# Queries and keys laid out chunk by chunk, and the row of maxima turned by VectorE

## The chip, the cores and the metric

The kernel runs on one core of one Trainium2 chip. What counts is the device time of one launch in microseconds, the median of the runs. A core has five engines with a queue of instructions each: TensorE (PE, with its weight loads shown apart as PEld), VectorE (DVE), ScalarE (ACT), GpSimd (POOL) and SyncE (SP), which here issues most DMAs. Sixteen DMA engines move what is issued.

## What is computed

Attention with hashed buckets comes first, and its output runs through a mixture of experts and a gated two-layer network. The change lies in the attention.

```python
B, H, S, D = q.shape                       # 2, 8, 768, 64
q_bits = (np.einsum('bhsd,dk->bhsk', q, proj) > 0).astype(np.int64)
k_bits = (np.einsum('bhsd,dk->bhsk', k, proj) > 0).astype(np.int64)
...
mask = q_bucket[:, :, :, None] == k_bucket[:, :, None, :]
scores = scale * np.matmul(q, k.transpose(0, 1, 3, 2))
scores = np.where(mask, scores, -1000000000.0)
scores = scores - np.max(scores, axis=-1, keepdims=True)
attn = np.exp(scores)
attn = attn / (np.sum(attn, axis=-1, keepdims=True) + 1e-09)
return np.matmul(attn, v).astype(np.float32)
...
x = _moe_ref(x=x, **moe_kwargs)
return _moe2_ref(x=x, **moe2_kwargs)
```

## The kernel before

There are 16 heads (batch times heads) of 768 queries and 768 keys each; 768 is six chunks of 128. For each head four tiles of 128 partitions by 768 columns hold the operands: `X` (queries in rows 0 to 63, 12 rows of bucket bits, and in row 76 the row of maxima), `K2` (keys and bits, with -1 in row 76), `Y` and `K1` (the high and low halves that make the product exact). Four such sets take turns.

Each head goes through two kinds of steps, both in chunks of 128.

`mx(n)` takes one chunk of queries as the stationary operand: two matmuls of 384 columns (line 425) give scores of 128 queries against all keys, and VectorE reduces each to a maximum per query (line 428). The stationary operand is `st["X"][0:76, c::NC]`, every sixth column, so chunk c holds the queries 6p + c for p from 0 to 127. After the sixth chunk one more reduction (line 431) writes the maxima of the head into `top`, with p on the partitions and c in the columns, and SP issues one DMA (line 432) that writes them into row 76 of `X` as one row in the order of the queries.

`scores(k)` takes a chunk of keys as the stationary operand: for each half of the queries (384 columns) line 442 multiplies the halves and line 443 adds the rest, with the row of maxima among it. ScalarE takes the exponential (line 444); it reads the 384 columns of PSUM with a stride of six, so that its output stands chunk by chunk. The tiles in PSUM that scores write into are two. Then ScalarE or VectorE rounds to half precision (`high`), GpSimd or VectorE forms the remainder (`low`), and `pv` (lines 470 to 472) multiplies both with v, 36 small matmuls at a time.

A loop over 96 steps (16 heads times 6) sets the order of everything: in step k come `scores(k)`, then `mx(k + 8)`, and in every odd step `pv` of two earlier steps. So in even steps the two matmuls of line 425 are followed directly by line 442 of the next step, and in odd ones by line 470. Work that comes once per head or per four heads is put between by a table of due steps: loads of queries and keys (`load_r`, line 348), loads of v (`load_v`, line 550) and their maxima on VectorE (`vmax`, line 554), the split into high and low parts (`prep`, lines 359 to 377, with six DMAs), the bucket bits (`bits`, line 398; `put_bits`, lines 383 and 384), and the products of v with the gate (`vgate`, line 531). Each engine and SP's queue run their instructions in that order; an SP instruction that waits holds back all later ones.

Of the kernel before, what the change touches and what calls it, by code (L numbers as in the profile page):

```python
# [9 lines left out]
F32 = mybir.dt.float32  # L10
F32R = mybir.dt.float32r
F16 = mybir.dt.float16
I32 = mybir.dt.int32
AF = mybir.ActivationFunctionType
# [5 lines left out]
P = 128  # L20
B, H, S, D = 2, 8, 768, 64
NH = B * H
BITS = 6
NC = S // P
HS = S // 2
# [17 lines left out]
SC = 2.0**-17  # L43
# [20 lines left out]
def moe_attention_kernel(ctx, tc, qk, v, vt, pj, wg, w1, w2, win, wout, out, cap):  # L64
    nc = tc.nc
    pe, act, dve, pool, sp = nc.tensor, nc.scalar, nc.vector, nc.gpsimd, nc.sync
# [3 lines left out]
    def opened(stack, name, bufs, side="left", **kw):  # L70
        return stack.enter_context(tc.tile_pool(name=name, bufs=bufs, side=side, reuse_waits="tile", **kw))

    def f32(t):
        return t.bitcast(F32)
# [229 lines left out]
    with ExitStack() as actx:  # L304
        pa = opened(actx, "pa", 1)
# [26 lines left out]
        pool.memset(b3, 3.0)  # L332
        rt, b_t = {}, {}
        nm = pa.tile([P, NH, NC], F32, tag="nm", name="nm")
        top = pa.tile([P, NH, NC], F32R, tag="top", name="top")
        mxs = [pa.tile([P, NC, 3], F32, tag=f"mx{i}", name=f"mx{i}") for i in range(2)]
        for t in mxs:
            dve.memset(t[:, :, 2:3], -0.5)
# [80 lines left out]
        def mx(n):  # L419
            h, c = divmod(n, NC)  # L420
            st = sets[h % 4]
            mm = mxs[h % 2]
            for n in range(2):
                ps = ps_m.tile([P, 512], F32, tag="m", name=f"psm{h}{c}{n}")
                pe.matmul(  # L425
                    ps[:, :HS], st["X"][0:76, c::NC], st["K2"][0:76, n * HS : (n + 1) * HS], start=True, stop=True
                )
                dve.tensor_reduce(out=mm[:, c, n : n + 1], in_=ps[:, :HS], axis=AX.X, op=ALU.max)  # L428
            if c == NC - 1:

                dve.tensor_reduce(out=top[:, h], in_=mm, axis=AX.X, op=ALU.max)
                sp.dma_start(out=f32(st["X"])[76:77, :].rearrange("o (p c) -> o p c", c=NC), in_=f32(top)[:, h])

        def scores(k):
            h, j = divmod(k, NC)
            st = sets[h % 4]
            pf = pf_t[k] = pt.tile([P, S], F32, tag="pf", name=f"pf{k}", bufs=4)
            kc = slice(j * P, (j + 1) * P)
            for n in range(2):
                ps = ps_t.tile([P, 512], F32, tag="t", name=f"pst{k}{n}")  # L440
                qc = slice(n * HS, (n + 1) * HS)
                pe.matmul(ps[:, :HS], st["K1"][:, kc], st["Y"][:, qc], start=True, stop=False)  # L442
                pe.matmul(ps[:, :HS], st["K2"][0:77, kc], st["X"][0:77, qc], start=False, stop=True)  # L443
                act.activation(  # L444
                    pf.rearrange("k (c n p) -> k c n p", c=NC, n=2)[:, :, n],
                    ps[:, :HS].rearrange("k (p c) -> k c p", c=NC), AF.Exp, scale=0.125 / SC / SC,
                )

        def high(k, eng):
            phi_t[k] = pt.tile([P, S], F16, tag="phi", name=f"phi{k}", bufs=6)  # L450
# [249 lines left out]
        st, r0 = sets[0], rt[0]  # L700
# [3 lines left out]
        for n in range(2):  # L704
            for i, t in enumerate(("X", "K2")):
                c = slice(n * HS, (n + 1) * HS)
                ps = (ps_m, ps_t)[i].tile([P, 512], F32, tag="mt"[i], name=f"psf{n}{i}")
                pe.matmul(
                    ps[D : D + 12, :HS], pj_sb[i * D : (i + 1) * D, 12 * i : 12 * i + 12], r0[i * D : (i + 1) * D, c],
                    start=True, stop=True,  # L710
# [10 lines left out]
        for n in range(NC):  # L721
            mx(n)
            if n in DOT:
                next(b0)
# [48 lines left out]
        for g in range(1, G):  # L773
            b = 4 * NC * (g - 1)
# [11 lines left out]
        for h in range(NH):  # L786
            k = NC * h + NC - 1 + LAG
# [52 lines left out]
        h = NH - 1  # L840
# [242 lines left out]
    def heat(n):  # L1083
# [21 lines left out]
        out=gates, in0=ps2[:, :, NW:], scalar=1.0 / LS, in1=gates, op0=ALU.mult, op1=ALU.add  # L1105
# [368 lines left out]
```

## Time and profile before

| | us |
|---|---|
| median of the runs (three) | 677.33 |
| lowest and highest run | 677.24, 678.81 |
| time of the profiled execution | 675.88 |
| its span | 674.1 |
| busy in the span: TensorE, VectorE, ScalarE, GpSimd | 638.4, 481.0, 426.6, 229.8 |

The profile is of one execution. The attention fills the first 240 us of the span; the rest are the experts and the two-layer network. A matmul's record reaches from its start to a modelled end, and records of neighbours overlap, so the distance between starts tells more than a duration. A busy share is an average over stages with different limits.

### The profile page before, as it was taken

Reading aid. Unit: us, or ns where it says so; the run is one execution under the profiler, and the core shown is the slowest. Engines: PE = TensorE matmul, PEld = TensorE weight load, DVE = VectorE, ACT = ScalarE, POOL = GpSimd, SP = SyncE. Lnnn points to the kernel's source line nnn. Section 1 sums busy time; section 2 is a strip of 40 time slices with the busy share of each in tenths; the row PEclk is TensorE's granted clock in tenths of the full one; section 3 lists DMA queues with packets and bytes.
Section 4 is the critical chain, followed back from the end, with each engine's and each line's share of the span. In section 5 each row is a group of like instructions: output and inputs, shape, how many; then the busy total and the mean of one; then the engine's idle time right before and its main releaser. Section 6 shows DMA issues by size and latency. Waiting matters only on the chain.

```text
span 674.1 us, 14367 instructions
## 1 busy us (share of the span) xinstructions
PE 638.4 (95%) x5518; PEld 479.7 (71%) x5518; DVE 481.0 (71%) x1038; ACT 426.6 (63%) x869; POOL 229.8 (34%) x199
## 2 busy tenths in 40 slices
PE   7899999999999769999999999999999999999894
PEld 2588889989899638999999997555555555555541
DVE  6768898898999957888888877888888452222320
ACT  3467778778787826776667765455445576555730
POOL 4339769769778233221077500000000021000011
PEclk9889999999999978999999999999999999999998
DMA  8584764764465065777677735443442011000011
GB/s 236 127 233 115 231 177 122 233 169 109 126 160 165 25 217 193 250 246 257 213 253 228 243 115 162 137 145 126 150 134 92 0 48 48 1 0 1 1 41 59
DMA packets 37840, 94.14 MB, mean 140 GB/s; under 512 B 7576, under 2 KB 13720, under 8 KB 37760
## 3 DMA queue, kind: packets, MB, share of 16 engines
q1 hardware_dynamic: 34672, 85.71, 42.7%
q0 software_dynamic: 2400, 7.36, 3.2%
q8 instruction: 46, 0.75, 0.4%
q14 instruction: 34, 0.28, 0.1%
q10 hardware_dynamic: 688, 0.03, 0.1%
HBM read 67.14 MB, written 6.29 MB: 109 GB/s over the span
## 4 chain that ended last, share of the span: by engine, by line
PE 75%; DVE 10%; DMA 6%; ACT 5%; issue 2%; SPq 0%; POOL 0%; POOLq 0%; ACTq 0%; DVEq 0%
PE psg L1249 16%; PE pso L1276 15%; PE psh L1006 11%; PE psy L1033 11%; PE psm L425 5%; PE pst L442 4%; PE pst L443 3%; DVE mx L428 2%; DMA out_dram<-os,inv 2%; PE psv L470 2%; PE psv L471 2%; PE psv L472 2%; PE psg L531 2%; DMA vr<-in_v_dram 1%; ACT junk L1203 1%
## 5 line engine op out<-in xcount | busy, mean ns | idle before, releaser
L458 POOL TENSOR_TENSOR plo<-pf,phi 128x768 f16<-128x768 f32 x86 | 147.1, 1736 | 60.4 <-ACT phi L452 24.9
L444 ACT ACTIVATE pf<-pst 128x384 f32<-128x384 f32 x192 | 83.5, 486 | 47.4 <-PE pst L443 45.7
L428 DVE TENSOR_REDUCE mx<-psm 128x1 f32<-128x384 f32 x192 | 96.3, 548 | 20.0 <-PE psm L425 19.7
L1291 POOL DMA_INDIRECT out_dram<-os,inv x12 | 12.1, 1008 | 270.8 <-DVE os L1283 244.5
L163 DVE SCALAR_TENSOR_TENSOR wl<-raw,wh 128x1024 f16<-128x1024 f32 (+1 forms) x68 | 82.7, 1218 | 6.3 <-ACT wh L157 5.2
L1249 PE MATMUL psg<-yTh,ch 128*128 128x512 f16 (+1 forms) x256 | 83.4, 326 | 3.2 <-DVE rl L1252 3.2
L1249 PE MATMUL psg<-yTl,ch 128*128 128x512 f16 (+1 forms) x256 | 83.4, 326 | 0.0
L1249 PE MATMUL psg<-yTh,cl 128*128 128x512 f16 (+1 forms) x256 | 83.4, 326 | 0.0
L1252 DVE SCALAR_TENSOR_TENSOR rl<-rl,psg 128x512 f32<-128x512 f32 x64 | 35.0, 551 | 64.4 <-ACT rl L1251 64.0
L442 PE MATMUL pst<-Y,K 128*128 128x384 f32 x192 | 75.2, 392 | 2.0 <-ACT pf L444 2.0
L1249 PEld LDWEIGHTS <-ch 128*128 128x128 f16 x512 | 50.0, 98 | 35.9
L452 ACT ACTIVATE phi<-pf 128x768 f16<-128x768 f32 x85 | 71.7, 844 | 1.9
L1276 PE MATMUL pso<-ch,gh 128*128 128x512 f16 x192 | 72.8, 379 | 0.0
L1276 PE MATMUL pso<-ch,gl 128*128 128x512 f16 x192 | 72.8, 379 | 0.0
L1276 PE MATMUL pso<-cl,gh 128*128 128x512 f16 x192 | 72.8, 379 | 0.0
L425 PE MATMUL psm<-K,X 76*128 76x384 f32 x192 | 66.8, 431 | 4.6 <-DVE mx L428 3.8
L157 ACT ACTIVATE wh<-raw 128x1024 f16<-128x1024 f32 (+1 forms) x68 | 67.6, 999 | 0.5 <-issue 0.4
L1276 PEld LDWEIGHTS <-gh 128*128 128x128 f16 x384 | 37.6, 98 | 42.3
L443 PE MATMUL pst<-X,K 77*128 77x384 f32 x192 | 66.5, 346 | 0.0
L1033 PE MATMUL psy<-hh,wl 128*128 128x224 f16 x256 | 66.3, 259 | 0.0
L1033 PE MATMUL psy<-hh,wh 128*128 128x224 f16 x256 | 66.3, 259 | 0.0
L1033 PE MATMUL psy<-hl,wh 128*128 128x224 f16 x256 | 66.3, 259 | 0.0
(231 smaller groups left out, 1495.2 us busy)
## 6 DMA issues: line engine op xcount, KB each, us to landing
raw<-in_w_dram SPq DMA_DIRECT2D x64, 512.0 KB
rc<-in_win_dram SPq DMA_DIRECT2D x16, 512.0 KB
rc<-in_wout_dram SPq DMA_DIRECT2D x16, 512.0 KB
r<-in_qk_dram SPq DMA_DIRECT2D x16, 384.0 KB
K<-hi SPq DMA_DIRECT2D x31, 192.0 KB
vr<-in_v_dram SPq DMA_DIRECT2D x4, 768.0 KB
vt<-in_vt_dram SPq DMA_DIRECT2D x8, 384.0 KB
Y<-hi SPq DMA_DIRECT2D x16, 192.0 KB
```

The lines of the kernel that those rows point to most:

```text
L163: dve.scalar_tensor_tensor(out=wl[e, i][:, c : c + n], in0=r, scalar=(S1, S2)[i // 2], in1=wh[e, i][:, c : c + n], op0=ALU.mult, op1=ALU.s ...
L425: pe.matmul(ps[:, :HS], st["X"][0:76, c::NC], st["K2"][0:76, n * HS : (n + 1) * HS], start=True, stop=True)
L428: dve.tensor_reduce(out=mm[:, c, n : n + 1], in_=ps[:, :HS], axis=AX.X, op=ALU.max)
L442: pe.matmul(ps[:, :HS], st["K1"][:, kc], st["Y"][:, qc], start=True, stop=False)
L443: pe.matmul(ps[:, :HS], st["K2"][0:77, kc], st["X"][0:77, qc], start=False, stop=True)
L444: act.activation(pf.rearrange("k (c n p) -> k c n p", c=NC, n=2)[:, :, n], ps[:, :HS].rearrange("k (p c) -> k c p", c=NC), AF.Exp, scale=0 ...
L452: act.activation(phi_t[k], pf_t[k], AF.Copy)
L458: eng.tensor_tensor(out=plo_t[k], in0=pf_t.pop(k), in1=phi_t[k], op=ALU.subtract)
L1006: pe.matmul(ps, l[:, c], r[:, k], start=n == 0, stop=n == 3 * KD - 1)
L1033: pe.matmul(ps, l, r, start=n == 0, stop=n == 3 * KF - 1)
L1249: pe.matmul(ps, l, x, start=n == 0, stop=n == 3 * KD - 1)
L1276: pe.matmul(po[blk][s], l, r, start=first and n == 0, stop=last and n == 2)
```

## The change

The host lays queries and keys out so that column c x 128 + p of a head is token 6p + c: each chunk of `X` is now contiguous, and v is loaded in the same order of keys. So the stationary operand of the maxima is `st["X"][0:76, c * P : (c + 1) * P]`, and the exponential reads PSUM and writes its tile contiguously. The row of maxima must now stand chunk by chunk as well. VectorE turns `top` in blocks of 32 x 32 into one of two tiles `tt`, after which chunk c of the block b lies in partition 32b + c; four DMAs of six partitions with 32 values each carry it into row 76. For that `top` is 26 columns wider and set to zero once.

```diff
-        top = pa.tile([P, NH, NC], F32R, tag="top", name="top")
+        top32 = pa.tile([P, NH * NC + 32 - NC], F32R, tag="top", name="top")
+        dve.memset(f32(top32), 0.0)
+        top = top32[:, : NH * NC].rearrange("p (h c) -> p h c", c=NC)
+        turned = [pa.tile([P, 32], F32, tag=f"tt{i}", name=f"tt{i}") for i in range(2)]
...
-                    ps[:, :HS], st["X"][0:76, c::NC], st["K2"][0:76, n * HS : (n + 1) * HS], start=True, stop=True
+                    ps[:, :HS], st["X"][0:76, c * P : (c + 1) * P], st["K2"][0:76, n * HS : (n + 1) * HS], start=True, stop=True
...
                 dve.tensor_reduce(out=top[:, h], in_=mm, axis=AX.X, op=ALU.max)
-                sp.dma_start(out=f32(st["X"])[76:77, :].rearrange("o (p c) -> o p c", c=NC), in_=f32(top)[:, h])
+                t = turned[h % 2]
+                dve.transpose(t, f32(top32)[:, h * NC : h * NC + 32])
+                rows = f32(st["X"])[76:77, :].rearrange("o (c b i) -> o b c i", c=NC, b=4)
+                for b in range(4):
+                    sp.dma_start(out=rows[:, b], in_=t[32 * b : 32 * b + NC, :])
...
-                act.activation(
-                    pf.rearrange("k (c n p) -> k c n p", c=NC, n=2)[:, :, n],
-                    ps[:, :HS].rearrange("k (p c) -> k c p", c=NC), AF.Exp, scale=0.125 / SC / SC,
-                )
+                act.activation(pf[:, qc], ps[:, :HS], AF.Exp, scale=0.125 / SC / SC)
...
-    qk = np.concatenate([q.transpose(0, 1, 3, 2), k.transpose(0, 1, 3, 2)], axis=2).reshape(NH, P, S)
-    vv = v.reshape(NH, NC, P, D).transpose(2, 0, 1, 3).reshape(P, NH * NC * D)
-    vt = v.reshape(NH // 2, 2, S, D).transpose(0, 1, 3, 2).reshape(NH // 2, P, S)
+    qk = np.concatenate([q.transpose(0, 1, 3, 2), k.transpose(0, 1, 3, 2)], axis=2).reshape(NH, P, P, NC)
+    qk = qk.transpose(0, 1, 3, 2).reshape(NH, P, S)
+    vv = v.reshape(NH, P, NC, D).transpose(1, 0, 2, 3).reshape(P, NH * NC * D)
+    vt = v.reshape(NH // 2, 2, P, NC, D).transpose(0, 1, 4, 3, 2).reshape(NH // 2, P, S)
```

The order of the instructions on TensorE, ScalarE and GpSimd stays as it was. It changes at two places per head. The first is SP's queue; here it is head 1, whose set holds `X_141`, before the change (a row is line, operation, out<-in and size):

```order
L348 DMA r_335<-in_qk_dram 128x768
L520 DMA vt_365<-in_vt_dram 128x768
L348 DMA r_367<-in_qk_dram 128x768
L432 DMA X_141<-top 1x128x6
L348 DMA r_448<-in_qk_dram 128x768
L376 DMA K_147<-lo_311 64x768
L377 DMA Y_146<-lo_311 64x768
L348 DMA r_485<-in_qk_dram 128x768
L550 DMA vr_547<-in_v_dram 128x1536
```

The same place of SP's queue in the changed kernel, whose lines stand a few further down:

```order
L351 DMA r_342<-in_qk_dram 128x768
L524 DMA vt_372<-in_vt_dram 128x768
L351 DMA r_374<-in_qk_dram 128x768
L439 DMA X_141<-tt_159 1x6x32 x4
L351 DMA r_459<-in_qk_dram 128x768
L379 DMA K_147<-lo_318 64x768
L380 DMA Y_146<-lo_318 64x768
L351 DMA r_496<-in_qk_dram 128x768
L554 DMA vr_558<-in_v_dram 128x1536
```

Where one DMA stood there are four, and the loads of r and v behind them keep their order.

The second place is VectorE's queue at the end of the maxima of head 1, before the change:

```order
L428 TENSOR_REDUCE mx_158<-psm_433 128x1
L428 TENSOR_REDUCE mx_158<-psm_436 128x1
L431 TENSOR_REDUCE top<-mx_158 128x6
L679 SCALAR_TENSOR_TENSOR vh_396<-vr_176,sc_353,vh_396 128x6x64
L683 MEMSET vh_396 128x6
```

And in the changed kernel:

```order
L431 TENSOR_REDUCE mx_161<-psm_440 128x1
L431 TENSOR_REDUCE mx_161<-psm_443 128x1
L434 TENSOR_REDUCE top<-mx_161 128x6
L436 STREAM_TRANSPOSE tt_159<-top 128x32
L683 SCALAR_TENSOR_TENSOR vh_403<-vr_179,sc_360,vh_403 128x6x64
L687 MEMSET vh_403 128x6
```

The transposition stands right behind the reduction that it reads, and nothing else moved.

## Rows read from the trace of the kernel before

**Rows 1.** Stretches of 10 us from 50 to 240: sum, busy us of each engine.

```profile
sum 190.00, PE 180.51 PEld 162.27 DVE 169.24 ACT 150.45 POOL 139.31; mean PE 9.50 PEld 8.54 DVE 8.91 ACT 7.92 POOL 7.33
```

**Rows 2.** Groups by line: shapes, count | busy us, mean ns | idle before, releaser.

```profile
L444 ACT ACTIVATE pf<-pst 128x384 f32<-128x384 f32 x192 | 83.5, 486 | 47.4 <-PE pst L443 45.7 <-POOL plo L458 0.8
...
L425 PEld LDWEIGHTS psm<-K,X 76*128 76x128 f32 x192 | 53.3, 313 | 12.3 <-DVE mx L428 8.7 <-ACT hi L359 2.1 <-issue 0.8
L443 PEld LDWEIGHTS pst<-X,K 77*128 77x128 f32 x192 | 37.3, 194 | 0.0
...
L992 ACT ACTIVATE xh<-psa 128x448 f16<-128x448 f32 x8 | 4.3, 543 | 10.2 <-PE psa L989 9.7
```

**Rows 3.** Timeline of TensorE's matmuls: start us, us, engine, line, operands, count.

```profile
148.40 0.62 PE L425 MATMUL psm<-K,X 76*128 76x384 f32 x2
148.86 0.43 PE L442 MATMUL pst<-Y,K 128*128 128x384 f32 x1
...
149.51 0.34 PE L443 MATMUL pst<-X,K 77*128 77x384 f32 x1
149.69 0.62 PE L425 MATMUL psm<-K,X 76*128 76x384 f32 x2
150.16 0.21 PE L470 MATMUL psv<-vh,phi 128*128 128x73 f16 x1
```

**Rows 4.** Timeline of ScalarE, the exponential of the same step.

```profile
148.30 0.49 ACT L444 ACTIVATE pf<-pst 128x384 f32<-128x384 f32 x1 [0.65 <-PE pst L443]
```

**Rows 5.** Timeline of the weight loads, the next one of line 442.

```profile
148.84 0.19 PEld L442 LDWEIGHTS pst<-Y,K 128*128 128x128 f32 x1
```

**Rows 6.** Chain of waits in order of time: start us, us, what.

```profile
54.72 0.45 PE psm L425 x2
...
123.25 0.55 PE psm L425
...
217.58 0.45 PE psm L425 x2
```

**Rows 7.** Groups by line, VectorE, the last reduction of a head.

```profile
L431 DVE TENSOR_REDUCE top<-mx 128x6 fp32r<-128x18 f32 x16 | 2.8, 172 | 0.5
```

**Rows 8.** Timeline of SP's queue around heads 1 and 13.

```profile
27.43 0.79 SPq L383 DMA_DIRECT2D X<-b  x1
...
35.57 0.53 SPq L432 DMA_DIRECT2D X<-top  x1
36.14 0.59 SPq L348 DMA_DIRECT2D r<-in_qk_dram  x1
...
38.68 0.56 SPq L550 DMA_DIRECT2D vr<-in_v_dram  x1
...
194.87 0.51 SPq L432 DMA_DIRECT2D X<-top  x1
```

**Rows 9.** Stretches: busy us, then granted clock, DMA share and GB/s.

```profile
28.00:30.00 2.00, 2.00 (x7) 1.28 (x5) 0.10 (x1) 1.18 (x2) 0.96 (x2) 0.50 1.06 218
...
32.00:34.00 2.00, 2.00 (x13) 1.83 (x13) 1.97 (x6) 0.00 (x0) 0.00 (x0) 0.90 0.07 25
...
36.00:38.00 2.00, 2.00 (x7) 1.36 (x6) 0.35 (x2) 1.93 (x4) 0.00 (x0) 0.50 1.02 373
```

**Rows 10.** Timeline of VectorE, the maxima of v.

```profile
48.67 1.01 DVE L554 TENSOR_REDUCE am<-vr 128x1 f32<-128x384 f32 x2 [1.39 <-DMA vr<-in_v_dram]
```

**Rows 11.** Stretches after the issue of head 15's row, columns as in rows 9.

```profile
219.10:220.20 1.10, 0.97 (x10) 0.64 (x6) 1.03 (x5) 0.71 (x3) 0.00 (x0) 1.00 0.00 0
220.20:220.50 0.30, 0.15 (x1) 0.15 (x2) 0.30 (x2) 0.30 (x2) 0.00 (x0) 1.00 0.26 10
```

**Rows 12.** Timeline of TensorE, the first reader of head 13's row.

```profile
198.34 0.34 PE L443 MATMUL pst<-X,K 77*128 77x384 f32 x1
```

**Rows 13.** Timeline of TensorE, the wait ahead of 26 us.

```profile
26.14 0.56 PE L425 MATMUL psm<-K,X 76*128 76x384 f32 x1 [1.68 <-DVE mx L428]
```

**Rows 14.** The page's row of TensorE's granted clock in 40 slices, in tenths.

```profile
PEclk9889999999999978999999999999999999999998
```

## Prediction

> **What bounds the kernel now.** I read the profile in this order: the table of engines by stretch, the groups of instructions by line, the timeline of TensorE in one step, and the chain of work that ended last. The change touches the attention stage alone, the first 240 us of 674.1. From 50 to 240 us TensorE is busy 180.5 us of 190, VectorE 169.2, ScalarE 150.5 [rows 1]. So TensorE sets the pace, with VectorE close behind, and a gain on TensorE counts only where nothing else stands ready to hold it.
>
> The operand that the change straightens is read by the weight loads of line 425, the scores for the maxima. Such a load takes 313 ns on average, against 194 ns for line 443, which loads the same width and one row more from contiguous columns [rows 2]. What this costs is read from starts of matmuls, since the matmul records overlap. Line 443 starts at 149.51, the pair of line 425 at 149.69, the next matmul, line 470, at 150.16 [rows 3]. A matmul of 384 columns behind a contiguous load thus takes 0.18 us and the pair takes 0.47, where two such steps would take 0.36. The median gaps of the stage (0.227 us within 80 pairs, 0.234 behind 40, against 0.180 behind 80 matmuls of line 443) give 0.10 per pair, and the 192 matmuls of the group [rows 2] make 96 pairs.
>
> **Half of the pairs gain nothing.** In the step before, the pair is followed directly by line 442 of the next scores (148.40 to 148.86, 0.46 as well [rows 3]). That matmul needs one of the two PSUM buffers of the scores, and the buffer comes free when the exponential of line 444 has read it. The exponential starts at 148.30 and takes 0.49, so it ends at 148.79 [rows 4], and the weight load of line 442 starts at 148.84, 0.05 later [rows 5]. In 31 of the 33 places where a pair of line 425 is followed by line 442 the distance from the exponential's end to that weight load is the same 0.05 us. So the exponential ends that wait, not the pair: behind a faster pair TensorE would wait for the same exponential. Only a pair followed by other work (the products with v, line 470, or a small product) passes its time on.
>
> **The weight loads, summed.** I go by the chain of waits, walked in windows of 20 us from the load that ends at 48.6 us to the end of the stage. On it 21 whole pairs are followed by line 470, the first at 54.72, the last at 217.58 [rows 6], and 6 by small products whose successors wait for nothing: 27 x 0.10 = 2.7 us. At 7 places the second matmul of a pair was released by VectorE and shows alone with 0.55 us, as at 123.25 [rows 6]; here the load itself lies open and the difference of the two loads counts, 7 x 0.12 = 0.8. At 7 places VectorE waits for the first matmul of a pair, 7 x 0.05 = 0.4. That is 3.9 us. Before 34 us the maxima of heads 0 and 1 go at VectorE's pace, and four or five of the same open places give 0.4. **Sum: -4.3 us.** The bounds are 2.7 (the whole pairs alone) and 6.3 (all 63 pairs that aren't followed by scores, 0.10 each).
>
> **The exponential.** It now reads PSUM contiguously instead of with a stride of six. Today's 384 elements take 486 ns; a contiguous read of 448 elements from PSUM by line 992 takes 543 [rows 2]. That is 57 ns for 64 elements, so the strided read is already no slower per element: I take 0.
>
> **The transpositions.** VectorE gets 16 of them, 128x32, and one memset at the start, under the wait for the first load. The nearest row is the small reduction just ahead (172 ns for 18 elements [rows 7]). With 14 elements more and the wait for its predecessor I take 0.2 us each, 3.2 us in all. None of the 16 places lies in a stretch where the chain runs over VectorE; what covers them is its slack of 11% [rows 1]. I put 0.2 us on the path, plus 0.5 because a TensorE that is 2% quicker runs into VectorE more often. Uncovered, the whole 3.2 would count.
>
> **Four DMAs for one on SP's queue.** Before, SP issues one DMA of 128 partitions for the row of maxima, 0.53 us; a DMA of 12 partitions (X<-b) takes it 0.79 [rows 8]. The new ones have 6 partitions each. I take 0.8 each because the 12-partition DMA is the nearest in shape, so three more and the longer first cost SP 0.83 x 4 - 0.57 = 2.7 us per head, spacing included; the lower bound is 3 x 0.57 = 1.7. [...]
>
> In the steady stage SP idles before and after each of these issues, so prep and loads move little. Two places remain.
>
> First, head 1. Its row is issued at 35.57, and behind it in SP's queue stand loads of r, from 36.14 on, and, at 38.68, the load of v for heads 4 to 7 [rows 8]. The DMA engines are empty before (0.07 busy at 32 to 34 us) and full after (1.02 at 36 to 38) [rows 9]. VectorE waits 1.39 us for that v, until 48.67 [rows 10], and everything follows from there. With r issued 2.7 us later, the engines finish what was issued before (some 0.8 MB at 373 GB/s, 2.1 us from 35.6 on) and stand empty for up to 2 us. Some engines are behind the others and have less of a gap. I take **+1.6 us**, bounds 0.5 (issue at the lower bound) and 2.7 (all of the delay).
>
> Second, the row's arrival. In a quiet queue nothing moves from 219.10, the issue of head 15's row, to 220.20, and all of it in the next 0.3 us [rows 11], so 1.35 us from issue to landing. After the change the last part is issued 2.5 us later and 0.2 for the transposition: 4.05 us in all. The first reader (line 443 of the head) comes 4.4 to 5.4 us after the issue for twelve of the heads 2 to 15, but 3.5 for head 13 (194.87 to 198.34 [rows 8, 12]) and 3.6 for head 15. Head 0 has 4.7, head 1 more. That is 0.5 us each for two heads, the second partly under ScalarE's work: **+0.6 us**, bounds 0 and 1.5.
>
> **The sum.** -4.3 + 0.2 + 0.5 + 1.6 + 0.6 = -1.4 us. The profiled execution took 675.88 us around its span of 674.1; it would take 674.5. It lies 1.45 below the median of the runs, 677.33, and I carry the same difference over: **675.9 us**, 0.2% below. A measurement of this kernel can tell about 0.3% from no change, 2.0 us, so a time below 675.3 counts as faster and one above 679.4 as slower.
>
> **Rivals.**
> *The v load isn't late.* If the DMA engines' backlog lasts over the gap, or the small DMAs are issued at 0.5 us, the term of 1.6 falls to about 0 and the arrival term to 0.1: -3.5, 673.8 us. For it: the engines are saturated for 12 us around. Against: before 35.5 they were empty, so no old backlog exists.
> [...]
> *The rows come late, and the kernel is slower.* The point from which it decides is 4.4 us between the reduction and the landing of the last part; twelve heads have 4.4 to 5.4. If a 6-partition issue takes 1.2 us, or other transfers hold a part back as long, the way is 5.3 us, and the stalls are about 0.8 us for four of these heads, 0.5 for two, 1.8 for heads 13 and 15 and 0.6 for head 0: 8.4 us instead of 0.6, and v another 1.1 later. Net +7.5, 684.8 us. Against it: the longest usual issue on SP's queue is the 0.79 of X<-b [rows 8].
> *The weight load doesn't shrink.* If the 313 ns come from the tile and not from the stride, 4.3 is lost and 2.9 stay: 680.2 us. Against: line 443 reads the same kind of tile in 194.
> *The exponential gains too.* [...] The rows speak against it. Were it 50 ns shorter, the 13 gated pairs on the chain would give 0.65 us: 675.2.
>
> **How the numbers follow.** Forecast 675.9 (own range 674.5 to 677.3): 0.48. V load not late: 0.20. Clock: 0.14. Rows late: 0.08. Weight load unchanged: 0.05. Exponential: 0.05. Faster takes the second case, the last, and a quarter of the forecast: 0.37. Slower takes the two slower cases: 0.13. The rest, 0.50, lies within 0.3%. The range that leaves out 2 in 10 runs from 673.5 (the v load in time, the sum at its middle) to 679.0 (clock down and the upper bounds of the v load).
>
> **What would show it.** Right: the weight loads of line 425 (428 after) fall to about 194 ns; pairs followed by line 470 take 0.36 and those followed by the scores still 0.46, with the weight load 0.05 after the exponential; SP issues take about 0.8; VectorE's wait for v grows from 1.39 to about 3. Wrong would be weight loads near 300, gated pairs that gain, a v load that lands by 48.7, or a first reader that waits for its row in more than two heads.

## The result, and the profile after

The changed kernel takes **686.02 us** (median of 4 runs, 682.92 to 688.37) against 677.29 for the kernel before in the same comparison: a ratio of 1.0135, 95% interval 1.0098 to 1.0171. It is slower by some 9 us where the forecast was 0.2% faster, and it lies outside the range. The profiled execution took 682.92 us around a span of 681.2; its counterpart before took 675.88 around 674.1, so the two traces differ by 7.1 us.

The page of the changed kernel: the row of TensorE's granted clock in 40 slices, and the chain of waits by engine.

```profile
PEclk9888999999998978999999999999999999999998
...
PE 71%; DVE 11%; DMA 8%; ACT 4%; issue 2%; SPq 2%; POOL 0%; POOLq 0%; DVEq 0%; ACTq 0%
```

The fourth slice (51 to 68 us) has an 8 that [rows 14] does not have there. DMAs and their issue on SP's queue hold 10% of the chain; before they held 6%, none of it for the queue.

The groups by line after (shapes, count | busy us, mean ns | idle before, releaser); they answer to [rows 2, 7].

```profile
L451 ACT ACTIVATE pf<-pst 128x384 f32<-128x384 f32 x192 | 83.6, 486 | 55.5 <-PE pst L450 55.2
...
L450 PE MATMUL pst<-X,K 77*128 77x384 f32 x192 | 67.0, 349 | 2.4 <-DMA X<-tt 2.3
...
L428 PEld LDWEIGHTS psm<-K,X 76*128 76x128 f32 x192 | 37.5, 201 | 18.2 <-DVE mx L431 14.2 <-ACT rs L375 1.3 <-DVE K L390 0.9
...
L436 DVE STREAM_TRANSPOSE tt<-top 128x32 f32<-128x32 f32 x16 | 3.4, 212 | 0.6
```

The weight load for the maxima fell from 313 to 201 ns, the exponential stayed at 486, a transposition takes 212: all three as forecast. The pairs behave as forecast too: of the 40 pairs from 48 to 225 us that are followed by line 474 (line 470 before), 24 take 0.35 to 0.36 us from their start to the next matmul, where the median before was 0.46, and those followed by the scores still take 0.45 (0.46).

```profile
48.58 0.52 PE L428 MATMUL psm<-K,X 76*128 76x384 f32 x2
48.94 0.21 PE L474 MATMUL psv<-vh,phi 128*128 128x73 f16 x1
```

But the weight load's idle time rose from 12.3 to 18.2 us, nearly all of the rise a wait for VectorE's maxima (8.7 before, 14.2 after), and the scores now wait for a row of maxima (X<-tt).

**Where the time went.** I took the start of the first matmul of the scores in each of the 96 steps from both traces (six steps are a head) and subtracted; I call the difference the lag. Up to step 8 the changed kernel is 0.3 us ahead; then the lag rises in four places and is nearly flat between them:

```
step      8     10     12     14     26     30     50     54     78     82     94
lag us -0.3   +1.6   +2.6   +3.0   +2.8   +4.0   +4.0   +4.7   +4.7   +7.3   +7.3
```

*Steps 8 to 14, the load of v.* SP's queue around head 1 after, where [rows 8] show one DMA for the row at 35.57 and the load of v at 38.68:

```profile
35.72 2.90 SPq L439 DMA_DIRECT2D X<-tt  x4
38.67 0.44 SPq L351 DMA_DIRECT2D r<-in_qk_dram  x1
...
40.44 0.61 SPq L351 DMA_DIRECT2D r<-in_qk_dram  x1
41.10 0.85 SPq L554 DMA_DIRECT2D vr<-in_v_dram  x1
```

The load of v is issued 2.4 us later. VectorE's timeline shows that it waits 2.29 us for it, where [rows 10] have 1.39, and TensorE then waits for VectorE, whose next work in its queue is the bucket bits (line 390; TensorE's wait there before, at line 398, and after):

```profile
50.24 1.01 DVE L558 TENSOR_REDUCE am<-vr 128x1 f32<-128x384 f32 x2 [2.29 <-DMA vr<-in_v_dram]
```

```profile
50.27 0.85 PE L398 MATMUL psb<-r,pj_sb 128*32 128x384 f32 x8 [0.43 <-DVE b L387]
```

```profile
51.83 0.85 PE L401 MATMUL psb<-r,pj_sb 128*32 128x384 f32 x8 [1.50 <-DVE b L390]
```

Five microseconds after TensorE starts again, its granted clock falls from 1.00 to 0.50 for 3.4 us, from 56.7 on. The stretches (busy us of each engine, then granted clock, DMA share, GB/s):

```profile
54.00:56.00 2.00, 1.98 (x16) 1.82 (x16) 1.93 (x6) 1.05 (x2) 2.00 (x3) 1.00 0.02 5
56.00:58.00 2.00, 2.00 (x27) 1.84 (x26) 1.35 (x4) 1.76 (x4) 2.00 (x2) 0.68 0.01 1
58.00:60.00 2.00, 2.00 (x22) 2.00 (x20) 0.63 (x3) 0.62 (x2) 2.00 (x2) 0.50 0.47 100
```

Some 2 us of the lag stand already ahead of the fall (the lag at step 11 is 1.8); the other 1.3 come with this stretch at a clock of 0.50.

*Steps 28 and 52, the loads of r.* Right behind the rows of heads 4 and 8 stand four loads of r. SP's queue at head 4, before and then after:

```profile
76.65 0.51 SPq L432 DMA_DIRECT2D X<-top  x1
77.20 2.01 SPq L348 DMA_DIRECT2D r<-in_qk_dram  x4
```

```profile
79.61 2.94 SPq L439 DMA_DIRECT2D X<-tt  x4
82.60 3.24 SPq L351 DMA_DIRECT2D r<-in_qk_dram  x4
```

The chain of waits of the changed kernel runs over them (start us, us, what):

```profile
83.55 1.82 SPq L351
...
85.41 6.32 DMA r<-in_qk_dram
...
91.78 0.83 PE psb L401 x2
```

The loads start 5.4 us later, 2.7 more than the lag of that place, and TensorE now waits for the last one: +1.2 us here, +0.8 at head 8.

*Step 80, the row of head 13.* The chain after:

```profile
199.37 0.18 DVE top L434
...
199.57 0.21 DVE tt L436
...
201.37 0.66 SPq L439
...
202.07 2.73 DMA X<-tt
...
204.94 0.41 PE pst L450
```

From the reduction's end (199.55) to the landing of the last part (204.80) pass 5.25 us, and its first reader waits 1.73; another stretch at a clock of 0.50 follows at 206.9. Together +2.5 us. The jump is not of this execution alone: `four_dmas_no_turn`, `kept_busy` and `v_on_pool` below, which have the same four DMAs and straight loads, have 2.3 to 2.5 us there.

### The profile page after: what moved, and what is told of

Read it like the earlier page. It is cut to its first block, busy times and chain, and to the rows that moved or that the text cites. A ratio compares the mean times of both kernels' runs of the same rounds, so it can differ in the third digit from the quotient of the medians.

```text
span 681.2 us, 14481 instructions
## 1 busy us (share of the span) xinstructions
PE 638.7 (94%) x5518; PEld 467.4 (69%) x5518; DVE 485.8 (71%) x1055; ACT 426.7 (63%) x869; POOL 227.0 (33%) x199
## 4 chain that ended last, share of the span: by engine, by line
PE 71%; DVE 11%; DMA 8%; ACT 4%; issue 2%; SPq 2%; POOL 0%; POOLq 0%; DVEq 0%; ACTq 0%
PE psg L1253 16%; PE pso L1280 15%; PE psh L1010 11%; PE psy L1037 11%; PE psm L428 4%; PE pst L449 3%; DVE mx L431 3%; PE pst L450 2%; DMA out_dram<-os,inv 2%; DMA r<-in_qk_dram 2%; ACT junk L1207 1%; PE psv L474 1%; PE psv L476 1%; PE psv L475 1%; DMA vr<-in_v_dram 1%
## 5 line engine op out<-in xcount | busy, mean ns | idle before, releaser
L1295 POOL DMA_INDIRECT out_dram<-os,inv x12 | 12.1, 1011 | 270.8 <-DVE os L1287 244.3
L476 PE MATMUL psv<-vh,plo 128*128 128x73 f16 x576 | 65.0, 197 | 1.8 <-DVE plo L462 1.8
```

Source lines behind the costliest of these rows:

```text
L476: pe.matmul(o, lo[:, cc], vv[:, j, 0:VA], start=False, stop=j == NC - 1, **grp)
```

## Experiments

The medians of the kernel before lay between 675.8 and 679.8 us on the chips used, so I compare ratios to the kernel before on the same chip, with 95% intervals. The changed kernel has only four runs, the others five to twelve, so a difference between its 1.0135 and another ratio is the less certain. A single trace holds clock falls that another execution may not have (the mean granted clock of the changed kernel's four runs is 0.958 to 0.975); the lag is used for places, the ratio for sizes. **Theory 1** is that the parts cost what the prediction said or less, and that the loss lies with the DMAs on SP's queue and what stands behind them; **theory 2** that VectorE paces; **theory 3** that the row's own late arrival, or the DMAs as such, are the loss.

### The parts of the change

`straight_old_row`: straight weight loads, no transposition, the old single DMA. The row then stands in another order than the queries, so that each query is shifted by another query's maximum; all work is still done.

```diff
-                t = turned[h % 2]
-                dve.transpose(t, f32(top32)[:, h * NC : h * NC + 32])
-                rows = f32(st["X"])[76:77, :].rearrange("o (c b i) -> o b c i", c=NC, b=4)
-                for b in range(4):
-                    sp.dma_start(out=rows[:, b], in_=t[32 * b : 32 * b + NC, :])
+                sp.dma_start(out=f32(st["X"])[76:77, :].rearrange("o (p c) -> o p c", c=NC), in_=f32(top)[:, h])
```

> The changed kernel with contiguous weight loads, but with the old row: no transposition, one DMA of 128 partitions per head (the row then holds the maxima in another order of the queries, which shifts the exponentials and leaves the attention as it is). Theory 1 (the prediction's: every open pair of the maxima passes 0.10 us on, and what the change lost it lost to the DMAs): 4.3 us below the kernel before, about 673.0. Theory 2 (VectorE paces the stage together with TensorE, so a quicker TensorE only waits for it): at most 1 us below, 676.3 to 677.3. In both the weight loads take about 190 ns.

Measured: **0.9955 (0.9926 to 0.9985)**, 3 us faster. The waits of TensorE and of its weight loads from 62 to 205 us show why it isn't the whole 4.3 (line, what it waited for: us, times, longest). Before:

```profile
PE psm L425 <- DVE mx L428: 2.1, 7, 0.4
PE pst L442 <- ACT pf L444: 0.8, 3, 0.3
```

```profile
PEld psm L425 <- DVE mx L428: 3.9, 7, 0.6
PEld pst L442 <- ACT pf L444: 2.9, 5, 0.6
```

With straight loads and the old row:

```profile
PE psm L428 <- DVE mx L431: 4.2, 10, 0.6
PE pst L445 <- ACT pf L447: 1.4, 3, 0.5
```

```profile
PEld psm L428 <- DVE mx L431: 8.4, 15, 0.9
PEld pst L445 <- ACT pf L447: 7.8, 22, 0.8
```

In this stretch the weight loads are busy 10.8 us less (126.65 to 115.83), the waits for VectorE grow from 6.0 to 12.6 and those for ScalarE from 3.7 to 9.2. The lag in this trace falls by only 0.8 us from step 8 to step 78; behind that a stretch of 10.2 us at a clock of 0.50, from 213.8 on, makes it the slowest of the twelve runs. Carried to 677.3 us the ratio is 674.3, between the two theories; its interval reaches from 672.3 to 676.3 and still holds theory 1's 673.0. That the open pairs pass on less than 0.10 us each rests on the traces.

`strided_new_row`: the four DMAs and the transposition, but the stationary operand strided again (`X[0:76, c::NC]`).

> The changed kernel with the stationary operand of the maxima read with a stride of six again (each chunk then holds other queries, so the row of maxima is in another order). Transpositions and four DMAs per head stay. Theory 1: what the straight loads gave is lost on top, 686.0 + 4.3 = 690.3. Theory 2: the straight loads gave nothing, so 685.5 to 687.

Measured: **1.0103 (1.0047 to 1.0159)**. The new row alone is about as slow as the whole change, and slower than this comparison's `before_plus_turn` (1.0001, below). The time is theory 2's, without its cause being shown; a gain of the straight loads beside the new row can't be read from the two overlapping intervals.

`four_dmas_no_turn`: as the changed kernel without the transposition; the four DMAs read `top` itself, so the row holds maxima of other queries.

> The changed kernel without the transposition: the four DMAs of six partitions read the tile of maxima itself (the row then holds other maxima). Theory 1 (the transpositions lie under VectorE's slack): 0.2 to 0.7 below the changed kernel, 685.3 to 685.8. Theory 2 (VectorE paces the stage): most of 16 x 0.21 = 3.4 us comes back, 682.6 to 683.6.

Measured: **1.0068 (1.0029 to 1.0107)**, against 1.0135 with the transposition. That is a little under theory 2's figure, and the intervals overlap: whether a transposition costs something beside straight loads, this run doesn't settle.

`before_plus_turn`: the kernel before with one transposition per head whose result nobody reads.

> The kernel before with one added transposition per head behind the last reduction, whose result nobody reads. Theory 1: 0.2 to 0.7 above the kernel before, 677.5 to 678.0. Theory 2: most of 3.4 us, 679.7 to 680.7.

Measured: **1.0001 (0.9964 to 1.0038)**. Beside the strided loads the transposition costs nothing that can be measured, as theory 1 says; the interval leaves room for 2.6 us. `strided_new_row` differs from this kernel in the four DMAs of the row and in the layout, which makes the exponential no shorter; so most of its loss is with the DMAs.

### Where the DMAs stand

`three_behind_row` adds three DMAs of no use behind the row of every head but the first, in the kernel before. `three_later` has the same loop not there but in the table of due steps, in a gap of the queue: at step 6h - 1.2, for head 1 at 9.2, behind its load of v. The edit of the first:

```diff
+        def three():
+            for i in range(3):
+                sp.dma_start(out=ddst[:, i], in_=dsrc)
...
                 sp.dma_start(out=f32(st["X"])[76:77, :].rearrange("o (p c) -> o p c", c=NC), in_=f32(top)[:, h])
+                if h > 0:
+                    three()
```

> The kernel before with three further DMAs of 6 partitions (24 values of no use to anyone, 768 bytes each) on SP's queue right behind the row of maxima of every head but the first; no transposition, strided loads, the row itself in time. Theory 1 (what stands behind the row on SP's queue is what costs: the loads of v and r): the lag rises by some 2 us at steps 9 to 14, by 1 to 1.5 at step 28 and 1 at step 52, and stays flat elsewhere: 4 to 5 us, ratio 1.006 to 1.008. Theory 3 (the row's own late arrival costs): no effect, since the row goes first: ratio 0.999 to 1.001.

> The kernel before with the same three further DMAs for every head but the first, put into the gap of SP's queue behind the loads of r, before the next prep; those of head 1 after the rush at step 9. The count of DMAs is the same as in three_behind_row, but no load waits for them. Theory 1: nothing or up to 0.7 us: ratio 1.000 to 1.001. If three small DMAs cost wherever they stand: as three_behind_row.

Measured: **1.0088 (1.0055 to 1.0121)** and **1.0009 (0.9978 to 1.0040)**. The row itself is issued as before in both, and TensorE's waits for it come to 0.8 and 0.2 us between 38 and 240 us, so theory 3 falls as the main cause: three DMAs in front of the loads cost 6 us, the same three in a gap nothing that can be measured. SP's queue in `three_behind_row`, and VectorE's wait there:

```profile
35.80 0.53 SPq L440 DMA_DIRECT2D X<-top  x1
36.37 2.15 SPq L342 DMA_DIRECT2D ddst<-dsrc  x3
...
40.97 0.57 SPq L560 DMA_DIRECT2D vr<-in_v_dram  x1
```

```profile
51.37 1.01 DVE L564 TENSOR_REDUCE am<-vr 128x1 f32<-128x384 f32 x2 [3.18 <-DMA vr<-in_v_dram]
```

The lag rises from 0 at step 8 to 6.7 at step 14 and is flat from there to step 82. The rise of 1 to 1.5 us at step 28 that I expected isn't there: the loads of r are issued 2.3 us late beyond the lag, and that is still in time.

### The load of v

`v_on_pool`: the changed kernel, with this one load issued by POOL on its own queue. `dummies_v_on_pool`: the same line in `three_behind_row`.

```diff
-            sp.dma_start(out=vr_t[g].rearrange("p h c d -> p (h c d)"), in_=v[:, g * n : (g + 1) * n])
+            (pool if g == 1 else sp).dma_start(out=vr_t[g].rearrange("p h c d -> p (h c d)"), in_=v[:, g * n : (g + 1) * n])
```

> The changed kernel, only the load of v for heads 4 to 7 asked for by POOL on its own queue (some 8 us earlier). Theory 1: the lag of 3.3 us at steps 9 to 14 goes, the later ones (steps 28, 52, 80) stay: 682 to 683.5 where the changed kernel has 686, ratio to before 1.006 to 1.009. If v is not what is late: 686, 1.013.

> three_behind_row (the kernel before, three useless DMAs behind every row) with the load of v for heads 4 to 7 on POOL's queue. Theory 1 (the late v, with what follows, is the loss): it vanishes nearly whole: ratio 0.998 to 1.001, where three_behind_row has 1.0088. Theory 5 (a shift of other loads counts as much): 1.004 to 1.008.

Measured: **1.0014 (0.9996 to 1.0033)**, 678.06 us, and **0.9994 (0.9955 to 1.0033)**. One DMA on another queue takes back 8 of the 9 us (5 to 11 by the two intervals), more than theory 1 expected, and the whole loss of the dummies. POOL issues it in a gap of its own, 8 us earlier than SP does in the kernel before:

```profile
30.57 0.59 POOL L554 DMA_DIRECT2D vr<-in_v_dram  x1
```

VectorE no longer waits for v, and the clock doesn't fall. With v on POOL the kernel before would be rid of its own wait of 1.39 us as well (the lag of `v_on_pool` drops by 1.2 us from step 8 to 14), so a little of the 8 us may not be the change's; the kernel before with v alone on POOL was not run, and with r moved as well it gained nothing (`before_r_early`, below: 1.0004). The stretch from 50 to 66 us (columns as above; the granted clock is the third number from the end) in the kernel before, the changed kernel, `four_dmas_no_turn`, `strided_new_row`, `three_behind_row`, `v_on_pool` and `dummies_v_on_pool`:

```profile
50.00:66.00 16.00, 15.30 (x173) 13.62 (x173) 14.03 (x35) 11.74 (x22) 13.90 (x10) 1.00 0.46 120
```

```profile
50.00:66.00 16.00, 14.11 (x143) 11.74 (x140) 12.52 (x31) 9.94 (x19) 12.16 (x8) 0.89 0.51 120
```

```profile
50.00:66.00 16.00, 12.77 (x77) 11.23 (x78) 8.15 (x20) 5.58 (x10) 8.10 (x5) 0.57 0.39 91
```

```profile
50.00:66.00 16.00, 14.06 (x118) 12.57 (x117) 8.80 (x22) 7.47 (x14) 8.12 (x6) 0.68 0.45 101
```

```profile
50.00:66.00 16.00, 13.84 (x118) 12.55 (x115) 9.13 (x21) 7.34 (x13) 8.63 (x6) 0.68 0.44 97
```

```profile
50.00:66.00 16.00, 15.51 (x179) 13.44 (x179) 13.62 (x35) 12.74 (x23) 14.30 (x10) 1.00 0.43 111
```

```profile
50.00:66.00 16.00, 15.92 (x198) 14.33 (x195) 13.28 (x34) 12.28 (x23) 13.78 (x10) 1.00 0.46 116
```

The waits at this place, all in us, with the lag that they and the clock leave behind:

| kernel | VectorE waits for v | TensorE waits behind it | clock at 0.50, 50 to 66 us | lag, step 8 to 14 |
|---|---|---|---|---|
| before | 1.39 | 0.43 | none | |
| changed | 2.29 | 1.50 | 3.4 | 3.3 |
| `strided_new_row` | 2.65 | 1.64 | 10.2 | 6.5 |
| `three_behind_row` | 3.18 | 2.16 | 10.2 | 6.7 |
| `four_dmas_no_turn` | 4.02 | 3.24 | 13.7 | 8.5 |
| `kept_busy` (below) | 4.46 | 2.28 | none | 4.1 |
| `three_later` | 2.41 | 1.46 | 3.4 | 2.4 |
| `before_plus_turn` | 0.63 | none | 6.8 | 3.1 |

In four of the five kernels with four small DMAs ahead of v the clock is at 0.50 for 3.4 to 13.7 us behind TensorE's wait (in `four_dmas_no_turn` from 51.9 us on, 1.3 us ahead of its end); in the traces of all seven kernels that issue v from POOL it doesn't fall at all between 42 and 62 us. At 13.7 us the fall itself loses up to 7 us of TensorE's work, an estimate from the clock of 0.50. The changed kernel's own trace has the shortest fall of the four and was the fastest of its four runs, which fits its median lying 3.1 us higher; those other runs have no trace, so this stays a reading. The last two rows warn against a single trace: both kernels issue v behind one DMA as before, both lose 2.4 and 3.1 us here with a fall of the clock (in `before_plus_turn` behind a wait of 0.68 us for X<-b), and neither is slower in the median. So the changed kernel's trace alone would not show that the late v is the loss; the two runs with v on POOL do.

`kept_busy`: the changed kernel, TensorE given 1.4 us more to do just ahead of the wait (chunk 17 of the maxima comes at step 9).

```diff
+            more = 8 if n == 17 else 0
             for n in range(2):
...
+                for _ in range(1 + n * more):
+                    pe.matmul(
+                        ps[:, :HS], st["X"][0:76, c * P : (c + 1) * P], st["K2"][0:76, n * HS : (n + 1) * HS], start=True, stop=True
+                    )
```

> The changed kernel; the second matmul for the maxima at step 9 is written nine times over the same tile (1.4 us of TensorE), just ahead of the wait for v. Nothing else is changed and the wait stays as long. If the clock falls because TensorE waits, and the fall is a good part of the loss: the half-clock stretch at 56.7 us is gone or shorter, and the time falls by 1.3 to 3 us to a ratio of 1.009 to 1.012. If the fall doesn't hang on that wait, or the loss is the wait alone: 1.013 to 1.015.

Measured: **1.0082 (1.0040 to 1.0123)**, and the trace has no fall there, although v came later still on that chip (VectorE waits 4.5 us):

```profile
52.00:54.00 2.00, 0.14 (x4) 0.14 (x8) 1.73 (x4) 0.00 (x0) 0.00 (x0) 1.00 0.52 123
...
58.00:60.00 2.00, 2.00 (x42) 1.84 (x41) 1.35 (x4) 1.73 (x4) 2.00 (x2) 1.00 0.01 1
```

That points the way theory 1 says, some 3.6 us for the fall and below the range expected, but the interval overlaps that of the changed kernel: likely, not shown. In the traces, too, this kernel's lag at the place is 2.6 us smaller than that of `three_behind_row`, whose TensorE waits as long (2.16 and 2.28 us) and whose clock falls. One sees as well that here a TensorE idle for 2.28 us was followed by no fall.

### Repairs that failed

Each of these was to take the late loads away in another manner. `loads_first` asks for v and r some steps earlier on SP's queue, ahead of the row (`'lv': 2.5`, loads of r at step `24 * (h // 4 - 1) - 3.5`); `before_loads_first` is the kernel before with that alone.

> The changed kernel; v for heads 4 to 7 and r for heads 8 to 15 are asked for one to three steps earlier, so that they stand ahead of the four DMAs of a row on SP's queue and not behind. Theory 1 (the late loads and the clock falls behind their waits are the loss): the lag of the trace at steps 10 to 14 (3.3 us), 28 (1.4) and 52 (0.8) goes, what is left is the late row of head 13: 680 to 681.5, ratio 1.004 to 1.006. Theory 3 (the DMAs cost by themselves, through the row's late arrival or by taking up the DMA engines): little changes: 684.5 to 686.5, ratio 1.010 to 1.013.

> The kernel before with the loads asked for earlier, nothing else: what the earlier loads are worth by themselves. Theory 1: at most the 1.39 us that VectorE waits for v: 676.0 to 677.0, ratio 0.998 to 0.9995. If the loads ahead of the row hold the row back: 677.5 to 679, ratio 1.000 to 1.003.

Measured: **1.0184 (1.0160 to 1.0207)** and **1.0119 (1.0099 to 1.0139)**: both slower, and by more than any of the theories had; the last branch of the second expectation names the cause, at a quarter of its size. The row now stands behind the loads. TensorE's timeline in `before_loads_first`:

```profile
43.21 0.41 PE L443 MATMUL pst<-X,K 77*128 77x384 f32 x1 [1.44 <-DMA X<-top]
...
87.83 0.44 PE L443 MATMUL pst<-X,K 77*128 77x384 f32 x1 [3.58 <-DMA X<-top]
```

A row of 3 KB, issued right behind four loads of 384 KB, comes 3.6 us too late at head 4, where the trace's lag rises by 4.3. It is issued at 80.98 and its first reader starts at 87.83, where [rows 11] have 1.35 us from issue to landing. So in these runs the place on the queue costs in both directions: small ahead of large delays the large one's issue (the load of v by 2.4 us in the changed kernel), large ahead of small delays the small one's landing (3.58 us of wait here).

`one_dma_loads_first` is `loads_first` with four 32x32 transpositions and one DMA for the row.

> Four transpositions and one DMA for the row, and the loads asked for earlier. Theory 1: no load is late with one DMA, so the earlier loads bring only what the earlier v brings to the kernel before as well (its own wait for v is 1.39 us): 674 to 676, ratio 0.995 to 0.998. Theory 3: as four_turns_one_dma.

Measured: **1.0179 (1.0149 to 1.0208)**, the same failure.

`loads_on_pool`: v and the loads of r for heads 8 to 15 on POOL's queue.

> The changed kernel with v for heads 4 to 7 and r for heads 8 to 15 asked for by POOL on its own queue at the same steps, so that the four DMAs of the row delay no load and no load stands ahead of them. Theory 1: the lag at steps 10 to 14, 28 and 52 falls away, 3 to 5 us less than the changed kernel, ratio 1.003 to 1.008 to before, if the row's parts aren't held up by the loads in the DMA engines. Theory 4 (row and loads share the DMA engines, whichever queue they come from): the row's last parts land behind the loads, waits for X at the first reader of heads 1, 4 and 8 take the place: as the changed kernel or worse, 1.012 to 1.018.

Measured: **1.0194 (1.0144 to 1.0245)**. The v part works (lag -0.4 at step 14, +3.0 in the changed kernel), but at heads 4 and 8 the lag jumps by some 7 and 4.5 us: at head 4 POOL issues the fourth load of r only behind another of its subtractions, at 82.82, and TensorE waits 2.1 us for r. The time is theory 4's or worse, but its mechanism is not what the trace shows at this place: TensorE's waits for X<-tt come to 2.3 us between 38 and 240 us, as in the changed kernel.

`v_pool_r_early`: v on POOL, three of each four loads of r six steps earlier on SP's queue. `before_r_early`: the kernel before with the same.

> The changed kernel with v for heads 4 to 7 on POOL's queue, and three of the four loads of r for heads 8 to 11 and 12 to 15 asked for six steps earlier, where SP's queue has a gap; the fourth stays behind the row. Theory 1: the lags at 10 to 14, 28 and 52 all go, the late row of head 13 stays: 679.5 to 681, ratio to before 1.002 to 1.006. If the earlier loads push the row back as in loads_first: above 684.

> The kernel before with v for heads 4 to 7 on POOL's queue and three loads of r six steps earlier: what the earlier loads bring without the change. Theory 1: the kernel before waits 1.39 us for v and not for r: 675.5 to 677, ratio 0.998 to 1.000.

Measured: **1.0065 (1.0033 to 1.0097)**, worse than with v alone, and **1.0004 (0.9986 to 1.0022)**. In the first the three loads now hold up what prep sends behind them (waits of TensorE); the kernel before with the same loads has no wait for K<-b:

```profile
PE psm L428 <- DMA K<-b: 3.1, 2, 1.6
```

### One DMA for the row

`four_turns_one_dma` turns each quarter of the partitions on its own into partitions 0 to 31, so that one DMA of 6 partitions writes the row, in the right order.

```diff
-        turned = [pa.tile([P, 32], F32, tag=f"tt{i}", name=f"tt{i}") for i in range(2)]
+        turned = [pa.tile([32, P], F32, tag=f"tt{i}", name=f"tt{i}") for i in range(2)]
...
-                dve.transpose(t, f32(top32)[:, h * NC : h * NC + 32])
-                rows = f32(st["X"])[76:77, :].rearrange("o (c b i) -> o b c i", c=NC, b=4)
                 for b in range(4):
-                    sp.dma_start(out=rows[:, b], in_=t[32 * b : 32 * b + NC, :])
+                    q = slice(32 * b, 32 * b + 32)
+                    dve.transpose(t[:, q], f32(top32)[q, h * NC : h * NC + 32])
+                sp.dma_start(out=f32(st["X"])[76:77, :].rearrange("o (c p) -> o c p", c=NC), in_=t[0:NC, :])
```

> The changed kernel with the row of maxima turned by four 32x32 transpositions, one for each quarter of the partitions, all into the partitions 0 to 31, so that one DMA of 6 partitions of 512 bytes writes the row. Theory 1 (the loss is the three further DMAs of each head and what stands behind them on SP's queue; VectorE's transpositions are nearly free): the straight loads' gain of 3.0 us seen with the old row, less about 1 for four transpositions: 675.0 to 676.5, ratio 0.996 to 0.999. Theory 2 (VectorE paces, every us that it gets counts): 16 x 4 x 0.13 us = 8 us on top of -3: 681 to 683, ratio 1.005 to 1.009.

> The changed kernel with four transpositions and one DMA for the row, and v for heads 4 to 7 on POOL's queue; r where it was. Theory 1: no load and no row late; the straight weight loads give 3 us, four transpositions take 1 to 2 back: 675 to 676.5, ratio 0.997 to 1.000. If the transpositions cost as much as the weight loads bring: 1.000 to 1.003.

> As v_pool_r_early, with four transpositions and one DMA for the row. Theory 1: no load and no row is late; the straight weight loads give 3, the earlier v 1, four transpositions take back 1 to 3: 674 to 676.5, ratio to before 0.996 to 0.9995. If VectorE's transpositions are the rest of the loss: 678 to 681, 1.002 to 1.006.

Measured: **1.0047 (1.0026 to 1.0068)**; with v on POOL **0.9992 (0.9956 to 1.0027)**; with three loads of r early as well **1.0032 (1.0013 to 1.0050)**. The groups by line of the first:

```profile
L438 DVE STREAM_TRANSPOSE tt<-top 32x32 f32<-32x32 f32 x64 | 12.8, 200 | 1.2
```

A quarter takes 200 ns where the whole took 212 and the expectation counted 130, an estimate that no run shows, so VectorE gets 9.4 us more. The first result misses theory 1's figure and lies at the lower edge of theory 2's; but its trace has v issued 0.7 us late, waits of 2.20 us for it and a clock fall, at 47.8. The second has no late load and no late row, hits theory 1's range and ends level with the kernel before; its lag falls by 1.2 us from step 8 to step 78, no less than that of `straight_old_row`, in spite of 12.8 us of transpositions. Its ratio is 0.0037 above that of `straight_old_row`, but the intervals overlap, so a price of the transpositions is not shown. The third misses theory 1 and lies in the range that its expectation gave to the transpositions; in its trace TensorE waits 2.2 us for what prep sends behind the early loads (K<-b and X<-hi), so this run doesn't single them out either. Of all kernels run, only `straight_old_row` is faster than the kernel before, and it puts the maxima against the wrong queries.

## Why the prediction was wrong

In the changed kernel's trace the sum of -1.4 us came out as +7.1. Four steps failed: the load of v, whose term ended with the wait (1.6 forecast; 3.3 in the trace, 8 in the medians); the weight loads, most of whose gain the trace doesn't show; the loads of r, put at nothing (2.0); and the row of head 13, priced too low (0.5 forecast, 2.5 in the trace).

**Weight loads, -4.3.** The load shrank as forecast (313 to 201 ns; expected about 194), and so did the pairs followed by products (0.46 to 0.36 us). What failed is the step from there to the path. In the traces the lag falls by 0.3 us (the changed kernel, steps 14 to 26, and nothing in its later flat stretches), 0.8 (`straight_old_row`, steps 8 to 78) and 1.1 (`v_on_pool`, steps 14 to 26); of the 3.9 us forecast from 48.6 us on, some 3 belong to steps 8 to 78, an estimate by the count of steps. The medians of `straight_old_row` give 3.0 us, and their interval, 1.0 to 5.0, holds the forecast too, so the size of the term stays open between the two. The weak step is the count of 27 pairs that pass their 0.10 on. Between 62 and 205 us of `straight_old_row` the loads got 10.8 us shorter and the waits for VectorE and ScalarE 12.1 us longer; the prediction had half of the pairs behind ScalarE, but for the open half it set against the gain only 0.5 us of VectorE. (The chain shows six places with 0.55 us, not seven; that is 0.1 us.)

**Exponential 0, transpositions +0.2.** The exponential is right: 486 ns both times. The transposition's length is right, 212 ns each, and so is its price beside strided loads (1.0001); beside straight loads the price stays open, as `four_dmas_no_turn` does not settle it.

**SP's issues.** Nearly right: 2.9 us for four with the spacing, 0.73 each (taken: 0.83).

**The load of v, +1.6.** The place was named, the wait has the forecast's sign and size (the load issued 2.4 us later, about 2 us of lag ahead of the fall, bounds 0.5 to 2.7; VectorE's wait grew to 2.29, not to about 3). The gap in the DMA engines came as well, with some engines behind the others: in the changed kernel their mean share falls from 0.57 at 38.0 to 38.1 us to 0.08 at 38.6 to 38.8 and 0.00 at 39.4 to 39.7, and is 0.84 in the tenth behind that. What failed is that the term ended with the wait. A clock fall behind it had a chance of 0.14; in four traces it is 3.4 to 13.7 us long at 0.50, by estimate 1.7 to 7 us of work, in a fifth (`kept_busy`) it is missing. The clock of 0.9 and more through the stage before [rows 14] speaks of waits as they were, not of one that is 1 us longer. With the load on another queue the ratio goes from 1.0135 to 1.0014: the late v and what follows it are most of the loss. How the 8 us of the medians divide into wait and clock is open: between the two profiled executions they are 3.5, and these were the fastest of the one kernel's runs and the slowest of the other's.

**"In the steady stage SP idles before and after each of these issues, so prep and loads move little."** Wrong at two of the heads: behind the rows of heads 4 and 8 stand four loads of r (77.20 before). They cost 1.2 and 0.8 us in this trace, and between nothing and 1.3 in the other traces with the four DMAs. To find them one has to go through what stands behind each of the sixteen rows, instead of the queue's idle time in general.

**The row's arrival, +0.6.** Head 13 was named, the price was too low: 5.25 us from the reduction to the landing instead of 4.05. The 1.35 us from issue to landing came from a quiet queue [rows 11]; at head 13 the last part took 2.73, with a load of 384 KB issued ahead of it. With the clock fall behind its wait that is 2.5 us instead of 0.5. Head 15 showed no such jump.

**The rivals.** "The rows come late" came near the time (684.8) by the wrong way, which is luck: it priced stalls at the first readers of nine heads, most of which didn't come, and `three_behind_row` loses 6 us with no new row on the queue. For a clock fall the chances have 0.14, and the range counts "clock down" at its upper end, 679.0. No run shows the price that stands in it; what the runs show is 1.3 us of lag with the fall in the changed kernel's own trace and, by the estimate above, 1.7 to 7 us of work in the four traces.

## What to carry to other kernels

Before adding small DMAs to a queue, go through every place where they will stand and write down what is issued behind them and by when it is needed; three DMAs of 768 bytes cost 6 us in front of loads and nothing measurable in a gap. A wait of one to three microseconds on the engine that sets the pace may be charged twice, as in four of the traces here (waits of 1.50 to 3.24 us, falls of 3.4 to 13.7 us): once as the wait and again as a clock fall behind it. So a stall that grows needs a range that reaches to both. When a gain comes from making the bound engine's work shorter, look at what it would wait for next: here loads that got 11 us shorter were followed by 12 us more of waits for two engines that were busy 80 and 90% of the time.

## What the runs showed of the hardware

The issue of four loads of r on SP's queue took 1.85 to 2.12 us at nine places where they stand right behind one DMA for the row, or behind it and three dummies; behind four DMAs for the row it took 2.83 to 3.70 us at seven of ten places; in the changed kernel, at head 4, one of the four took 1.82 and its neighbours 0.42 to 0.44. What holds it is open. A 32x32 transposition takes VectorE as long as one of 128x32 (200 and 212 ns), so the quarters are not cheaper. And moving three or four loads of 384 KB to another part of a queue was seldom free: in the kernels with all loads first, and in `v_pool_r_early`, something small behind them was needed sooner than they were. Only the kernel before with three loads six steps earlier lost nothing (1.0004).
